# Three small moves of DMA issues in a fused attention-and-MLP kernel: V's parts one per step, w1's quarters on two queues, m0 on a third

## Chip, cores and metric

One Trainium2 chip, one core. The metric is device time in microseconds (us), the median of several executions of the whole program. The span of a profile is shorter than the time of the same execution (before: span 1509.4 us, time 1511.56 us), so spans are compared with spans and times with times.

## The reference, cut to what matters

```python
xn = layernorm(x)                                  # x: 1 x 2048 x 1024, bf16
out = x + A(xn, mem0, Wq, Wk, Wv, Wo, seg_len=32)  # attention by segments of 32 tokens,
                                                   # 32 heads of 128, 8 memory rows handed on
        + B(xn, w1, w2, w3, w4)                    # MLP block
# B begins with  h = gelu(layernorm(xn) @ w1)      # w1: 1024 x 1024
# A, per segment: q, k, v from [mem, xs]; p = softmax(mask(q k^T)); o = p v; o @ Wo
#   mem0: 8 x 1024
```

Everything is on the path somewhere, but TensorE's matrix products are nearly the whole time. The three things that the change touches are loads: `w1` and the first tiles of `x`, `mem0` (called m0 in the kernel), and the tile V, which holds the values of one block of segments for four heads.

## The kernel before

Three places issue the DMAs in question; SyncE (`nc.sync`) issues all of them.

```python
# 1. start: x tiles (128 x 1024) and w1 in quarters, all on SyncE's queue
load_x(0)
for c in range(4):
    nc.sync.dma_start(w1_sb[:, 2 * c:2 * c + 2, :], w1_v[:, 2 * c:2 * c + 2, :])
    if c in (0, 2):
        load_x(1 + c // 2)
# ... statistics, normalisation, transposes of x tile 0 on TensorE, then
def stage1_k(xn2T):              # first product: walks w1's quarters in order
    for k in range(KT):          # KT = 8, two k to a quarter
        if k == KT - 2:
            tr(1, 0); tr(1, 1)   # transposes of x tile 1, ahead of the last quarter
        for co in range(KT):
            nc.tensor.matmul(pss[co // 4][:, co % 4, :], w1_sb[:, k, ...], xn2T[:, 0, k, :], ...)

# 2. between the MLP's stages: 8 rows of memory, ahead of w4
m0 = ring.tile([M, D], BF16, tag="nsq", bufs=1)
nc.sync.dma_start(m0[:], A_mem0[0])

# 3. attention: V's two to four parts in one go
def load_values(B, V, hg):
    for n, i0 in ...:
        nc.sync.dma_start(V[0:w, i0:i0 + k, :], ...)        # token rows, the big part
        if b == 0:
            nc.sync.dma_start(V[96:106, 0, :], Vr_d[0:10, cs_])
        nc.sync.dma_start(V[w:w + n, i0:i0 + k, :], ...)    # memory rows
# ... the attention loop emits one entry of `loads` per step of TensorE work:
loads.append(lambda B=B, V=V, hg=hg: load_values(B, V, hg))
# ... and between the steps each tile's probabilities Pn are transposed by DMA, on SyncE too:
nc.sync.dma_start_transpose(PTr, Pn[:rows]...)              # PT, read by the product with V
```

The last three output stores go to SyncE, SyncE and ScalarE; then a branch follows that is not taken, and the program ends.

```python
for o, q in zip(rest[-3:], (nc.sync, nc.sync, nc.scalar)):
    o.queue = q                  # piece() ends with  queue.dma_start(out_v[...], ot[...])
...
with tc.If(cond > 0):            # line 891 before, 896 after
```

Each DMA that SyncE or ScalarE issues is given one of eight completion counters in turn, in program order, the two engines sharing the eight (read from the semaphores of the DMA instructions in the traces). No line of the source names them.

## Time and profile before

| | before |
|---|---|
| time, 3 runs | 1510.99 us (1510.84 to 1512.13) |
| span of the profile | 1509.4 us |
| PE busy | 1501.7 us |
| waits of PE that the profile lists | 2.9 us |
| of which on DMA: w1 0.8 us, PT 0.4 us | 1.2 us |
| last matmul's end to the end of the span | 4.73 us |

Read it from the top down: PE is busy to within 8 us, and 4.7 of these lie behind its last instruction. The lines for the rows in the middle are in the prediction. For the last row, here is the timeline of all engines at the end of the kernel before (start in us, duration, engine, line, operation; the bracket is the engine's idle time before it). SyncE's last output store at 1501.67 is left out.

```profile
1501.78 2.89 PE L720 MATMUL pso<-wo_sb,oX 128*128 128x256 bf16 x25
...
1504.71 0.42 DVE L726 TENSOR_TENSOR ot<-pso,Rt 128x256 bf16<-128x256 f32 x1 [3.07 <-PE pso L720]
1505.17 0.38 ACTq L727 DMA_DIRECT2D out_dram<-ot  x1
```

The chain at the end is: last matmul, one addition, ScalarE's issue of the last store at 1505.17.

### The profile page before, as it was taken

To read this page: it belongs to the slowest core of one execution; us is meant where nothing else is said; L and a number is where in the kernel's file an instruction comes from. 1 tells how busy PE (TensorE), PEld (TensorE's weight loads), DVE (VectorE), ACT (ScalarE), POOL (GpSimd) and SP (SyncE) were. 2 spreads that over 40 slices of the span, in tenths; PEclk is the share of its full clock that TensorE was granted. 3 is DMA by queue.
4 is the path that set the end of the run, shared out by engine and by line. 5 is a ranking of instruction groups with operands and counts; after the bars stand their busy time and mean duration, and the time that the engine had idled before them with its cause. 6 is when DMAs were issued, how large, how long until landed. Compare 5 with 4: busy or idle time off the path is not lost.

```text
span 1509.4 us, 24313 instructions
## 1 busy us (share of the span) xinstructions
PE 1501.7 (99%) x9834; PEld 803.5 (53%) x9834; DVE 544.8 (36%) x1136; ACT 502.8 (33%) x1140; POOL 175.4 (12%) x245
## 2 busy tenths in 40 slices
PE   9999999999999999999999999999999999999998
PEld 7744444445444444444466645664665455545555
DVE  8382230100020212222146624651664166516641
ACT  6533103013012011111256614650663266416620
POOL 5241020211111221100000010001000100010001
PEclk9999999999999999999999999999999999999999
DMA  9599752353355777522399957992997299918911
GB/s 304 160 252 338 219 177 88 133 203 112 125 165 145 196 252 253 209 98 84 126 229 249 239 129 183 249 240 66 250 244 200 79 223 230 210 60 213 205 46 51
DMA packets 305363, 272.93 MB, mean 181 GB/s; under 512 B 156006, under 2 KB 272264, under 8 KB 305248
## 3 DMA queue, kind: packets, MB, share of 16 engines
q1 hardware_dynamic: 283360, 190.44, 50.7%
q0 software_dynamic: 21744, 80.83, 15.5%
q8 instruction: 79, 1.29, 0.4%
q14 instruction: 36, 0.29, 0.1%
q10 hardware_dynamic: 144, 0.07, 0.0%
HBM read 190.08 MB, written 45.29 MB: 156 GB/s over the span
## 4 chain that ended last, share of the span: by engine, by line
PE 98%; DMA 1%; SPq 0%; issue 0%; DVE 0%
PE ps L662 30%; PE pso L720 15%; PE ps L601 15%; PE ps L542 13%; PE ps L568 13%; PE ps L400 4%; PE ps L318 3%; PE psS L677 2%; PE psO L701 2%; PE ps L860 1%; PE ps L492 1%; DMA PT<-Pn 1%; DMA w_sb<-in_B_w_dram 1%; PE gps L471 0%; PE ps L457 0%; PE ps L295 0%
## 5 line engine op out<-in xcount | busy, mean ns | idle before, releaser
L662 PE MATMUL ps<-hTb,wt 128*128 128x396 bf16 (+2 forms) x2528 | 484.8, 342 | 0.0
L662 PEld LDWEIGHTS <-wt 128*128 128x128 bf16 x2528 | 236.8, 98 | 175.4
L601 PE MATMUL ps<-wt,xT 128*128 128x512 bf16 x1024 | 221.2, 379 | 0.0
L720 PE MATMUL pso<-wo_sb,oX 128*128 128x512 bf16 (+1 forms) x992 | 210.0, 372 | 0.0
L542 PE MATMUL ps<-xn3T,w_sb 128*128 128x512 bf16 x896 | 196.2, 379 | 0.0
L568 PE MATMUL ps<-w_sb,h3T 128*128 128x512 bf16 x896 | 195.5, 379 | 0.0
L601 PEld LDWEIGHTS <-xT 128*128 128x128 bf16 x1024 | 100.2, 98 | 120.8
L543 ACT ACTIVATE h3T<-ps 128x512 bf16<-128x512 f32 x112 | 66.9, 597 | 290.3 <-PE ps L542 289.4
L720 PEld LDWEIGHTS <-oX 128*128 128x128 bf16 x992 | 96.3, 98 | 107.4
L664 ACT CAST KT<-ps 128x462 bf16<-128x462 f32 (+2 forms) x160 | 81.8, 511 | 202.9 <-PE ps L662 198.9
L568 PEld LDWEIGHTS <-h3T 128*128 128x128 bf16 x896 | 87.0, 98 | 103.4
L542 PEld LDWEIGHTS <-w_sb 128*128 128x128 bf16 x896 | 86.6, 98 | 102.1
L683 DVE TENSOR_REDUCE sums<-sm 99x4 f32<-99x396 f32 (+2 forms) x176 | 97.6, 555 | 114.5 <-ACT sm L681 114.5
L666 ACT ACTIVATE QT<-ps 128x462 bf16<-128x462 f32 (+2 forms) x160 | 84.0, 525 | 120.4 <-PE ps L662 106.3
L603 ACT CAST Vs<-ps 128x512 bf16<-128x512 f32 x64 | 37.5, 586 | 233.2 <-PE ps L601 233.2
L679 DVE TENSOR_TENSOR sm<-psS,c_mask_reg_sb 99x396 f32<-99x396 f32 x152 | 86.7, 571 | 72.4 <-PE psS L677 72.2
L607 DVE CAST Vs<-ps 128x512 bf16<-128x512 f32 x64 | 44.3, 692 | 171.6 <-PE ps L601 171.6
L681 ACT ACTIVATE sm<-sm 99x396 f32<-99x396 f32 (+2 forms) x176 | 93.0, 528 | 34.5 <-DVE sm L679 27.6
L689 DVE TENSOR_TENSOR Pn<-sm,rs 99x396 bf16<-99x396 f32 (+2 forms) x176 | 98.9, 562 | 6.9 <-DMA PT<-Pn 1.0
L727 POOL DMA_DIRECT2D out_dram<-ot x30 | 16.4, 547 | 698.6 <-DVE ot L726 692.7
L569 DVE TENSOR_TENSOR R<-ps,R 128x512 f32<-128x512 f32 x32 | 21.9, 689 | 176.0 <-PE ps L568 160.5
L726 DVE TENSOR_TENSOR ot<-pso,Rt 128x512 bf16<-128x512 f32 (+1 forms) x33 | 22.2, 675 | 170.3 <-PE pso L720 166.2
(122 smaller groups left out, 1047.8 us busy)
## 6 DMA issues: line engine op xcount, KB each, us to landing
wt<-in_A_Wq_dram SPq DMA_DIRECT2D x76, 512.0 KB
wt<-in_A_Wk_dram SPq DMA_DIRECT2D x76, 512.0 KB
wt<-in_A_Wv_dram POOLq DMA_DIRECT2D x24, 1024.0 KB, 6.3
V_scratch<-Vs SPq DMA_DIRECT2D x32, 512.0 KB
V<-V_scratch SPq DMA_DIRECT2D x40, 384.0 KB
R_scratch<-x POOLq DMA_DIRECT2D x16, 512.0 KB, 4.1
R<-R_scratch SPq DMA_DIRECT2D x16, 512.0 KB
R_scratch<-R POOLq DMA_DIRECT2D x16, 512.0 KB, 3.6
```

Source lines behind the costliest of these rows:

```text
L542: nc.tensor.matmul(ps[:].rearrange("p (n t) -> p n t", t=P), w3_sb[:, k, f * P:(f + 1) * P], xn3T[tb][:, :, k, :], start=(k == 0), stop=(k ...
L543: nc.scalar.activation(h3T[:, f, :], ps[:], ACTF.Gelu_apprx_tanh)
L568: nc.tensor.matmul(ps[:], h3T[:, f, j * P:(j + 1) * P], w4_sb[:, f, ch * 512:(ch + 1) * 512], start=(f == 0), stop=(f == FT - 1))
L601: nc.tensor.matmul(ps[:], xT[:, m4 * 4 + j, k, :], wv[:, k, :], start=(k == 0), stop=(k == KT - 1))
L662: nc.tensor.matmul(ps[:, :nb], w[:, k, hh * P:(hh + 1) * P], B["hT"][:, k, :nb], start=(k == 0), stop=(k == KT - 1))
L664: nc.scalar.copy(dst[:, hh, :], ps[:, :nb])
L666: nc.scalar.mul(dst[:, hh, :], ps[:, :nb], scale)
L679: nc.vector.tensor_tensor(sm[:T, :, :T], S3, t["mask"][:].unsqueeze(1).to_broadcast((T, 4, T)), op=ALU.add)
L681: nc.scalar.activation(e[:T, :, :T], sm[:T, :, :T], ACTF.Exp, scale=LN2)
L683: nc.vector.tensor_reduce(ss, e[:T, :, :T], axis=AX.X, op=ALU.add)
L689: nc.vector.tensor_tensor(Pn[:T, :, :T], e[:T, :, :T], rs[:T, :].unsqueeze(2).to_broadcast((T, 4, T)), op=ALU.mult)
L720: nc.tensor.matmul(self.ps[:, :self.w], self.oX[0][:, h, self.oX[1] + self.gl * P:self.oX[1] + (self.gl + 1) * P], wo_sb[:, h, self.cc], s ...
```

## The change

Its intent: let two queues bring w1 in, so that fewer loads stand one behind the other at the start; take a small load off SyncE ahead of w4; and put V's parts at separate steps, so that a transpose of probabilities that TensorE will wait for does not queue behind all of them.

```diff
-for c in range(4):
-    nc.sync.dma_start(w1_sb[:, 2 * c:2 * c + 2, :], w1_v[:, 2 * c:2 * c + 2, :])
-    if c in (0, 2):
+for c, q in ((0, nc.scalar), (2, nc.scalar), (1, nc.sync), (3, nc.sync)):
+    if q is nc.sync:
         load_x(1 + c // 2)
+    q.dma_start(w1_sb[:, 2 * c:2 * c + 2, :], w1_v[:, 2 * c:2 * c + 2, :])
@@
-nc.sync.dma_start(m0[:], A_mem0[0])
+nc.gpsimd.dma_start(m0[:], A_mem0[0])
@@
-def load_values(B, V, hg):          # issues V's parts itself
+def value_loads(B, V, hg):          # returns one function for each part
+    def add(dst, src):
+        out_.append(lambda: nc.sync.dma_start(dst, src))
     ...                             # the same parts, nc.sync.dma_start(...) -> add(...)
+    return out_
@@
-    loads.append(lambda B=B, V=V, hg=hg: load_values(B, V, hg))
+    loads += value_loads(B, V, hg)
```

TensorE's instruction order is the same in both programs, and no arithmetic is added or removed.

More of the change, by code (lines that the diff above doesn't have):

```diff
@@ L645, in block_setup @@
             return dict(b=b, tiles=tl, nb=nb, ntok=ntok, hT=hTb)
-        def load_values(B, V, hg):
-            b, cs_ = B["b"], slice(hg * 512, (hg + 1) * 512)
+        def value_loads(B, V, hg):
+            b, cs_, out_ = B["b"], slice(hg * 512, (hg + 1) * 512), []
+            def add(dst, src):
+                out_.append(lambda: nc.sync.dma_start(dst, src))
             for n, i0 in ((3, int(b == 4)),) + (((2, 4 if b == 3 else 0),) if b > 2 else ()):
@@ L651, in load_values @@
                 r, w = SEG * t["seg"], SEG * n
-                nc.sync.dma_start(V[0:w, i0:i0 + k, :], V_d[r:r + w * k, cs_].rearrange("(t p) c -> p t c", p=w))
+                add(V[0:w, i0:i0 + k, :], V_d[r:r + w * k, cs_].rearrange("(t p) c -> p t c", p=w))
                 if b == 0:
-                    nc.sync.dma_start(V[96:106, 0, :], Vr_d[0:10, cs_])
+                    add(V[96:106, 0, :], Vr_d[0:10, cs_])
                     i0, k, t = 1, 3, B["tiles"][1]
-                nc.sync.dma_start(V[w:w + n, i0:i0 + k, :], Vr_d[t["r0"]:t["r0"] + n * k, cs_].rearrange("(t j) c -> j t c", j=n))
+                add(V[w:w + n, i0:i0 + k, :], Vr_d[t["r0"]:t["r0"] + n * k, cs_].rearrange("(t j) c -> j t c", j=n))
+            return out_
         def proj(B, w, hh, dst, scale):
```

## The prediction

> **What bounds the kernel now.** I read the head of the page first, with its busy row, clock row and DMA queues.
>
> ```profile
> span 1509.4 us, 24313 instructions
> ...
> PE 1501.7 (99%) x9834; PEld 803.5 (53%) x9834; DVE 544.8 (36%) x1136; ACT 502.8 (33%) x1140; POOL 175.4 (12%) x245
> ...
> PEclk9999999999999999999999999999999999999999
> ...
> q1 hardware_dynamic: 283360, 190.44, 50.7%
> ...
> q10 hardware_dynamic: 144, 0.07, 0.0%
> ```
>
> TensorE (PE) is busy 1501.7 of 1509.4 us, at full granted clock in every slice. The DMA queue of ScalarE (q10) carries almost nothing, 0.07 MB; nearly all of SyncE's and hence of the kernel's loads go through q1. Busy is not the same as fast, so the second view is PE's timeline in the middle of the MLP, where each row is a run of matmuls that nothing interrupts.
>
> ```profile
> 122.30 48.51 PE L542 MATMUL ps<-xn3T,w_sb 128*128 128x512 bf16 x224
> 170.65 48.51 PE L568 MATMUL ps<-w_sb,h3T 128*128 128x512 bf16 x224
> ```
>
> From the start of the first run to the start of the second are 48.35 us for 224 matmuls of 512 columns: 215.8 ns each. There is no slack inside a busy stretch. The page's mean of 379 ns for the same matmuls counts the overlap of neighbours twice and must not be multiplied by their count. So only PE's idle time can be won, and the third view, who PE waited for, holds all of it (total us, times, longest).
>
> ```profile
> PE warm L335 <- DVE wz L329: 1.4, 1, 1.4
> PE ps L308 <- DMA w_sb<-in_B_w_dram: 0.8, 2, 0.5
> PE psO L701 <- DMA PT<-Pn: 0.4, 1, 0.4
> PE ps L295 <- DVE xn L274: 0.3, 1, 0.3
> ```
>
> The listed waits sum to 2.9 us. Of these the first, 1.4 us, is program start, and the last, 0.3 us, is the normalisation of the first x tile. What DMA can be blamed for is 0.8 us on w1 (named w_sb here; line L308 is the first stage-1 product, which walks w1's quarters in order) and 0.4 us on one transposed probability tile PT. The rest of the 7.7 us between busy and span is the end: PE's last matmul ends at 1504.7 us, and output store and final semaphores follow until 1509.4. The change touches none of that. The fourth view is PE's timeline at the start (start, duration; the bracket is the idle time before).
>
> ```profile
> 6.57 0.72 PE L295 MATMUL ps<-c_ident_sb,xn 128*128 128x128 bf16 x8 [0.29 <-DVE xn L274]
> 7.43 1.96 PE L308 MATMUL ps<-xn2T,w_sb 128*128 128x128 bf16 x32
> 9.69 1.07 PE L308 MATMUL ps<-xn2T,w_sb 128*128 128x128 bf16 x16 [0.30 <-DMA w_sb<-in_B_w_dram]
> 10.59 0.61 PE L295 MATMUL ps<-c_ident_sb,xn 128*128 128x128 bf16 x8
> 11.72 1.07 PE L308 MATMUL ps<-xn2T,w_sb 128*128 128x128 bf16 x16 [0.52 <-DMA w_sb<-in_B_w_dram]
> ```
>
> Sixteen matmuls belong to one quarter of w1, so quarters 1 and 2 run at 7.43 without a wait, the third waits 0.30 us and the fourth 0.52 us (before it PE does the second tile's transposes, 10.59). The fifth view asks whether those two quarters are late because they were issued late or because the DMA engines were full (last two columns: mean share of the 16 engines busy, GB/s).
>
> ```profile
> 2.00:4.00 2.00, 2.00 (x6) 0.67 (x5) 0.53 (x1) 0.24 (x2) 0.61 (x1) 1.00 0.98 226
> 4.00:6.00 2.00, 2.00 (x7) 0.65 (x5) 1.19 (x4) 0.00 (x0) 0.66 (x1) 1.00 0.91 349
> 6.00:8.00 2.00, 1.57 (x21) 1.08 (x20) 1.74 (x4) 0.99 (x4) 0.07 (x1) 1.00 1.01 340
> 8.00:10.00 2.00, 1.70 (x31) 1.52 (x29) 1.11 (x4) 0.21 (x1) 1.14 (x4) 1.00 1.06 409
> ```
>
> The engines are 91 to 106% busy from 2 us on, but deliver only 226 GB/s in the first window and about 345 in the next two, against 409 later. SyncE had issued the fourth quarter by 4.7 us (issue at 4.01, 0.68 us long), seven microseconds before PE got it. Late data, then, not late issue. The last view is SyncE's own timeline ahead of the single PT wait (PE at 797.12).
>
> ```profile
> 786.97 1.15 SPq L652 DMA_DIRECT2D V<-V_scratch  x1
> 788.16 0.70 SPq L654 DMA_DIRECT2D V<-Vmem_scratch  x1
> 788.92 0.26 SPq L656 DMA_DIRECT2D V<-Vmem_scratch  x1
> 789.28 2.61 SPq L692 DMA_TRANSPOSE PT<-Pn  x1
> ```
>
> The transpose at 789.28 is the one that PE waits for; its tile Pn was finished at 787.2 (VectorE started it at 786.64 for 0.57 us), and SyncE was then busy with the three parts of V.
>
> **What the Trainium skill says.** "DMA: Bandwidth & Descriptors", section "Issuing engines are not separate DMA queues": DMAs started from different engines run on the same 16 DMA engines and interleave, and a second issuer saves only the issue time. The windows above agree as far as they can: full engines while one queue issues. The same page, "Queues, rings and completion order": each DMA engine takes turns between the queue rows that have work, packet by packet. No trace of the kernel before shows two loaded hardware queues, so the sharing below is an estimate resting on that sentence. "TensorE: Matmul & The Clock Gate", section "Wait — 56ns, not 53.3ns?", gives 215.7 ns between warm 512-column matmuls; the trace has 215.8, so PE's stretches are at their floor.
>
> **The change part by part.** Comparing the two programs with line numbers aligned, PE's instruction order is identical and so are ScalarE's except for two DMA issues at its head; no arithmetic is added or removed. The base of the sum is therefore the old time, 1510.99 us.
>
> (1) w1 on two queues. On one queue the order is x0, q0, x1, q1, q2, x2, q3 (x tile 256 KB, quarter 512 KB), so these are complete after 256, 768, 1024, 1536, 2048, 2304 and 2816 KB. Adding up the trace's packet records on q1 gives when each amount was across: 2.96, 4.90, 5.71, 7.29, 8.68, 9.33, 10.62 us; PE sees a quarter about 1.0 us later (q2: 8.68 to 9.69; q3: 10.62 to 11.72). After the change ScalarE issues q0, q2 and SyncE x0, x1, q1, x2, q3. With equal turns x0 is complete at 512 KB, q0 and x1 at 1024, q1 and q2 together at 2048, x2 at 2304, q3 at 2816. Thus q2, x2 and q3 gain nothing, while x0 and q1 lose.
> - Same delivery as before: x0 lands at about 3.9 us (between 2.96 at 256 KB and 4.90 at 768) instead of 2.96. The chain that it feeds (statistics from 3.47, transposes at 6.57, first product at 7.43) moves to about 8.4. q1, at 2048 KB, is visible at 9.7. Then q1 and q2 run 9.7 to 11.7, the transposes to 12.2, and q3, there since 11.7, starts at 12.2 instead of 11.72: plus 0.5 us.
> - Two queues fill the start: if from 1.8 us (first packet 1.77) the engines deliver 400 GB/s, 2048 KB are across at 7.0 and 2816 KB at 9.0 us. Both w1 waits, 0.82 us, vanish; x0 costs some 0.15 us. Minus 0.7 us.
> The slow start consists of packets that took 400 to 1000 ns instead of the usual 84, at the first touch of x0 and w1, and these may partly overlap on two queues. I put the mean at minus 0.1 us. ScalarE's two issues cost about 0.9 us at its head (SyncE's took 0.42 and 0.47 each), before its 1.28 us table load; it is first needed at 7.01, so this is beside the path.
>
> (2) m0 moved to GpSimd's queue: 0.62 us of issue leave SyncE at 130.5 us. The w4 loads behind it feed products from 170.65 us, and PE does not wait there. VectorE swaps one xr sum (2.35 us for two) with the first R addition (180.49 us); the PSUM buffer that this addition frees is wanted again at 194.8 us (176.7 plus three groups of 6.05), so zero.
>
> (3) V's parts one per step. Same bytes, same number of DMAs; only which of them stands between two PT transposes changes. Of the row of three, the two small ones (0.70 + 0.26 us) go behind the next transpose, so a transpose leaves up to 1.0 us earlier. The one wait is 0.36 us, so the gain is at most that; but the 384 KB part stays ahead of it on the same queue, and the issue-to-use time was 7.7 us, most of it moving data. I count minus 0.15. V itself comes a few steps later, some 1.5 us each; the products that read it are scheduled 10 to 12 us after their scores, so no new wait is expected.
>
> Sum: 1510.99 - 0.1 + 0 - 0.15 = 1510.7 us.
>
> **The rivals.** (a) The x0 chain and q1 become the first wait: for it speaks the byte count, against it only the slow first packets. It makes 1511.3 to 1511.5. If PE's idle stretch before the first product also brought the clock down (the warm-up matmuls, 4.91 us for 12, ran at about half speed), another 1 to 2 us: 1513. (b) Everything is won: w1 waits and PT wait gone, 1510.99 - 0.82 - 0.36 = 1509.8. For it speaks that 226 GB/s leaves room; against it that the engines were already marked busy. (c) The shifted transposes make new waits of a few tenths in the first block, where loads and transposes share a queue at over 100% busy share: 1511 to 1512. No rival reaches 2%, which is 30 us; all PE idle time of the old trace together is a tenth of that.
>
> **Range and chances.** The effects span -1.2 to +1 us, and the three old runs alone spread from 1510.84 to 1512.13. I say 1510.7 us, range 1509.3 to 1512.3. Faster by over 2%: 0.01; within 2%: 0.98; slower by over 2%: 0.01.
>
> **What would show it.** In the new profile PE stays at about 1501 us busy. Step 1: q10 carries about 1.1 MB; PE's waits on w_sb either shrink below 0.8 us in total (fill) or a wait appears at the second quarter and the first product moves from 7.43 past 8 us (sharing). If the time between first packet and 2816 KB is unchanged at about 8.8 us, queues do not add delivery. Step 3: the PT wait of 0.4 us goes or stays below 0.4, and no psO wait over 0.5 us is new. I would be wrong if PE's total idle grew by more than 2 us, or if matmul cadence changed anywhere.

## The result, and the profile after

| | before | after |
|---|---|---|
| time, 6 runs each | 1511.05 us (1510.12 to 1512.14) | 1510.68 us (1510.15 to 1511.5) |
| ratio, 95% interval | | 0.9997 (0.9984 to 1.001): same |
| span of the profile | 1509.41 us | 1508.11 us |

Here and below a ratio is the mean time of one kernel's fast runs over that of the other's in the same rounds, so not quite the ratio of the medians that are quoted.

The time is where the prediction put it. The traces say whether for its reasons. First the head of the page of the changed kernel.

```profile
span 1508.1 us, 24241 instructions
...
PE 1498.3 (99%) x9762; PEld 803.5 (53%) x9834; DVE 544.6 (36%) x1136; ACT 501.9 (33%) x1140; POOL 175.6 (12%) x246
...
q10 hardware_dynamic: 688, 1.11, 0.2%
```

ScalarE's queue q10 now carries 1.11 MB, as intended. PE's busy time is 3.4 us lower, but this is no gain: 72 matmul records are missing (9762 against 9834, while the weight loads are 9834 in both). PE's totals can't be compared here, only times at which a given weight load starts. Done so, by the number of the weight load, the 1.30 us between the spans divide up as follows.

| stretch | before, us | after, us | difference |
|---|---|---|---|
| start to the first product's first weight load | 7.07 | 7.69 | +0.62 |
| from there to the first weight load after the first product | 5.50 | 4.32 | -1.18 |
| near 31.6 us (x tile 7's transposed tile lands later) | | | +0.16 |
| attention, the stretch of the PT wait (787.6 to 798.3) | 10.68 | 10.72 | +0.04 |
| last matmul's end to the end of the span | 4.73 | 3.80 | -0.94 |

The first two rows are step 1 of the prediction. PE's timeline at the start of the changed kernel:

```profile
7.19 0.72 PE L295 MATMUL ps<-c_ident_sb,xn 128*128 128x128 bf16 x8 [0.51 <-DVE xn L274]
8.04 2.84 PE L308 MATMUL ps<-xn2T,w_sb 128*128 128x128 bf16 x48
10.72 0.61 PE L295 MATMUL ps<-c_ident_sb,xn 128*128 128x128 bf16 x8
11.17 1.06 PE L308 MATMUL ps<-xn2T,w_sb 128*128 128x128 bf16 x16
```

The first product starts at 8.04 instead of 7.43 us, and then runs three quarters (x48) and the fourth (x16) without a wait on w1. VectorE's first use of x tile 0 tells why it starts later. Here is that row, of before and then of after:

```profile
3.47 0.69 DVE L259 BATCH_NORM_STATS2 st<-xt 128x6 f32<-128x512 bf16 x1 [2.15 <-DMA xt<-in_A_x_dram]
```

```profile
4.08 0.69 DVE L259 BATCH_NORM_STATS2 st<-xt 128x6 f32<-128x512 bf16 x1 [2.76 <-DMA xt<-in_A_x_dram]
```

x tile 0 arrives 0.61 us later, because it now shares the DMA engines with the first quarter of w1: by 4.0 us the packet records have 256 KB, all of x tile 0, across on SyncE's queue and 296 KB on ScalarE's. And the windows of the changed kernel (the last two columns are DMA share and GB/s):

```profile
2.00:4.00 2.00, 2.00 (x6) 0.69 (x5) 0.00 (x0) 1.25 (x2) 0.60 (x1) 1.00 0.93 275
4.00:6.00 2.00, 2.00 (x6) 0.68 (x5) 1.72 (x4) 0.00 (x0) 0.04 (x1) 1.00 1.06 404
6.00:8.00 2.00, 1.40 (x10) 0.51 (x9) 1.28 (x4) 0.38 (x2) 0.68 (x1) 1.00 1.03 383
```

275, 404 and 383 GB/s stand against 226, 349 and 340 before. On these two traces alone one would say: two queues fill the engines better, and this pays for the later x tile. The experiments test that.

Step 3, SyncE's timeline ahead of the PT transpose:

```profile
786.84 1.24 SPq L651 DMA_DIRECT2D V<-V_scratch  x1
788.19 2.10 SPq L697 DMA_TRANSPOSE PT<-Pn  x1
790.33 0.83 SPq L651 DMA_DIRECT2D V<-Vmem_scratch  x2
```

The transpose leaves at 788.19 instead of 789.28, right behind the big part of V, and the two small parts come after it. This is what the change meant to do. PE's wait there shrinks from 0.36 to 0.13 us, but a wait of 0.10 us on a Wq tile appears at 789.6 us.

The last row was not in the prediction. The end of the changed kernel:

```profile
1501.74 2.57 PE L725 MATMUL pso<-wo_sb,oX 128*128 128x256 bf16 x22
...
1504.35 0.42 DVE L731 TENSOR_TENSOR ot<-pso,Rt 128x256 bf16<-128x256 f32 x1 [3.07 <-PE pso L725]
1504.80 0.37 ACTq L732 DMA_DIRECT2D out_dram<-ot  x1
```

The same chain, with the same durations, 0.36 us earlier. But the span ends 1.30 us earlier: from the issue of the last store to the end it takes 3.30 us instead of 4.24. The records of SyncE's sequencer, which the timeline does not print, show how. SyncE checks the eight completion counters one after the other before the program may end (start of each check in us, one of SyncE's waits on a semaphore, counted here from 0 in the order of the checks; the last line is the end of the span):

```
before              after
1506.77 counter 0   1501.92 counter 0
1506.87 counter 1   1502.02 counter 1
1506.96 counter 2   1502.11 counter 2
1507.37 counter 3   1502.19 counter 3
1507.46 counter 4   1502.26 counter 4
1507.54 counter 5   1502.34 counter 5
1507.62 counter 6   1502.88 counter 6
1507.69 counter 7   1506.39 counter 7
1509.41 end         1508.11 end
```

Before, the last store is counted on counter 0. SyncE waits at its first check until that store has landed, 1.60 us after its issue (1505.17 to 1506.77; the counter's last update is recorded at 1506.75), and has the other seven checks still ahead of it. After, the last store is on counter 7: seven checks are done while TensorE is still at work, the eighth waits for the store (1504.80 to 1506.39, 1.59 us), and what follows is the same as before, 1.72 us. The seven checks are 0.92 us. The reason is the giving out in turn: m0 on GpSimd's queue means one DMA fewer among those of SyncE and ScalarE, so every later one gets the counter before its own, and the last store moves from 0 to 7.

That the store is felt only 1.6 us after its issue fits the Trainium skill, "Perfetto Trace Analysis", section "DMA Instruction — HWDGE (DVE, Sync)": the counter is written after the data write is confirmed, which can take surprisingly long when the target is HBM.

### The profile page after: what moved, and what is told of

It reads as the page before. It is cut to its first block, busy times and chain, and to the rows that moved or that the text cites. A ratio compares the mean times of both kernels' runs of the same rounds, so it can differ in the third digit from the quotient of the medians.

```text
span 1508.1 us, 24241 instructions
## 1 busy us (share of the span) xinstructions
PE 1498.3 (99%) x9762; PEld 803.5 (53%) x9834; DVE 544.6 (36%) x1136; ACT 501.9 (33%) x1140; POOL 175.6 (12%) x246
## 3 DMA queue, kind: packets, MB, share of 16 engines
q10 hardware_dynamic: 688, 1.11, 0.2%
## 4 chain that ended last, share of the span: by engine, by line
PE 97%; DVE 1%; DMA 1%; issue 0%; POOL 0%; ACT 0%; SPq 0%; POOLq 0%
PE ps L667 30%; PE pso L725 15%; PE ps L601 15%; PE ps L542 13%; PE ps L568 13%; PE ps L400 4%; PE ps L318 2%; PE psS L682 2%; PE psO L706 2%; PE ps L865 1%; PE ps L492 1%; PE gps L471 0%; PE ps L457 0%; DMA wt<-in_A_Wq_dram 0%; DVE st L262 0%
```

## The experiments

The theory after this reading: (T1) the end is the only lasting effect, 0.93 us, and follows from the last store's counter; (T2) two queues deliver w1 faster, net minus 0.5 us at the start; (T3) V's parts save a few tenths. The rival to all three: differences of half a microsecond between two traces are chance, since a trace is one execution. Eleven runs were made, two of them of the unaltered kernels; all were correct, and all were timed in rounds beside the kernel before. "End" is always from the last matmul's end to the end of the span; "x0" is when VectorE first reads x tile 0; "first product" is the time of the first weight load after it, 12.57 us before and 12.01 us after.

### One part at a time

**w1_only.** The kernel before with the first hunk alone.

```diff
+for c, q in ((0, nc.scalar), (2, nc.scalar), (1, nc.sync), (3, nc.sync)):
```

> The kernel before with only w1 on two queues; m0 stays with SyncE, V in one step. The program gives the last store DMA completion counter 0 of the 8 that SyncE and ScalarE share, as in the kernel before (counter 7 in the changed kernel). Three-causes theory (head, V, end are separate): first stage-1 product at 8.0 us, no w1 wait on PE, PE 0.56 us ahead at the first single-matmul product and 0.40 us ahead after tile 7; the PT wait near 797 stays at 0.2 to 0.5 us; the end from PE's last matmul to the last instruction stays at 4.7 us; span about 1509.0. Rival (w1's queues did it all): span 1508.1, end 3.8 us. Rival (end is chance): end anywhere between 3.8 and 4.7.

Measured: 1511.5 us (1510.57 to 1512.45) against 1511.18 for the kernel before, ratio 1.0001 (0.9987 to 1.0014). End 4.725, as before. x0 at 3.86, first product done at 11.78, PE's lead over the first trace 0.79 us there and 0.63 us at the last matmul: more than the changed kernel's 0.56 and 0.36. In time there is no gain at all, so PE's lead over that one trace is not yet a lead over the kernel before.

**m0_only.** The second hunk alone.

```diff
-nc.sync.dma_start(m0[:], A_mem0[0])
+nc.gpsimd.dma_start(m0[:], A_mem0[0])
```

> The kernel before with only m0 moved to GpSimd's queue. It has one hardware-queue DMA less, so the last store takes completion counter 7, which SyncE checks last. Three-causes theory: PE's timeline as before to within 0.05 us (w1 waits 0.30 and 0.52, PT wait 0.36, last matmul ends at 1504.7), but the end shrinks from 4.73 to about 3.8 us, span 1508.5, time 0.9 us below before. Rival (moving m0 is worth nothing, as the prediction counted): end 4.7 us, span 1509.4.

Measured: 1510.02 us (1509.6 to 1511.52), ratio 0.9992 (0.9979 to 1.0006). End 3.791, as T1 says. The expectation for PE missed: w1 is still on one queue here, and yet PE has no wait on w1, and the first product is done at 11.69, earlier than with two queues. So the 0.82 us of w1 waits belonged to the first trace, not to the kernel.

**v_only.** The third hunk alone.

```diff
-    loads.append(lambda B=B, V=V, hg=hg: load_values(B, V, hg))
+    loads += value_loads(B, V, hg)
```

> The kernel before with only V's parts at separate steps. Three-causes theory: head as before, end 4.7 us; near 797 the 0.36 us PT wait shrinks to about 0.1 but a wait on Wq or on the next PT near 790 of 0.1 to 0.3 us takes its place, so PE's last matmul ends within 0.1 us of 1504.67. Prediction's step 3: the wait only shrinks, last matmul 0.15 us earlier (up to 0.36). Span 1509.2 to 1509.5 in either.

Measured: 1510.56 us (1510.03 to 1512.11), ratio 0.9993 (0.9979 to 1.0006). End 4.730. Two rows of PE's timeline show what V's parts did in this run:

```profile
790.32 0.86 PE L667 MATMUL ps<-hTb,wt 128*128 128x403 bf16 x4 [0.60 <-DMA wt<-in_A_Wq_dram]
...
797.63 0.34 PE L706 MATMUL psO<-PT,V 99*128 99x99 bf16 x4 [0.25 <-DMA PT<-Pn]
```

The PT wait is 0.25 instead of 0.36, and a wait of 0.60 on a Wq tile is new. PE also waited 0.36 us at 39 us and 0.20 us at 1291 us, places that do not stand in the first trace. Both expectations for PE missed: its last matmul ends at 1505.53, 0.86 us later than in the first trace and not 0 to 0.36 us earlier, and the span is 1510.26.

**again.** The changed kernel, unaltered.

> The changed kernel unaltered, to see what repeats. If the differences of the two traces are the program's and not the run's: first product at 8.0, PE 0.56 ahead then 0.40, last matmul at 1504.3, end 3.8 us, all within 0.1 us of the first trace. If they are chance, they differ by as much as 0.5 us. Time against before, 5 rounds: minus 0.9 to minus 1.3 us if the trace's span gain (1.30 us) is what the clock measures, minus 0.4 or less if not.

Measured: 1509.56 us (1509.34 to 1510.54), ratio 0.9988 (0.9974 to 1.0001). End 3.794, x0 at 4.01, first product done at 11.94: these repeat to 0.07 us. But the last matmul ends at 1504.81, 0.50 us later than in the first trace of the same kernel, because PE waited 0.56 us at 39 us. The expectation of 0.1 us was missed by that: one trace does not tell half a microsecond in PE's total. The time lies 1.6 us below the kernel before in the same rounds, more than the 0.9 to 1.3 us expected.

### The same kernel twice, and the counter by itself

**before_again.** The kernel before, unaltered, timed against itself.

> The kernel before unaltered, timed against itself: what chance alone does. If the w1 waits (0.30 and 0.52 us) of its first trace belong to the program, they are here again within 0.1 us. If they belong to that run (the two kernels with w1 on one queue that ran since, m0 alone and V alone, showed none), they are absent, the 2 to 8 us windows deliver over 340 GB/s and PE is 0.7 to 0.9 us ahead of the first trace at the end of the first product. The end stays at 4.73 us in both. Ratio of times 1.000, and its interval shows what three rounds can tell.

Measured: 1511.36 us (1511.02 to 1511.87) against 1510.93, ratio 1.0001 (0.9985 to 1.0016). End 4.730. PE's timeline and the windows of this second trace of the kernel before:

```profile
7.50 2.84 PE L308 MATMUL ps<-xn2T,w_sb 128*128 128x128 bf16 x48
10.18 0.61 PE L295 MATMUL ps<-c_ident_sb,xn 128*128 128x128 bf16 x8
10.88 1.07 PE L308 MATMUL ps<-xn2T,w_sb 128*128 128x128 bf16 x16
```

```profile
2.00:4.00 2.00, 2.00 (x6) 0.67 (x5) 0.45 (x1) 0.24 (x2) 0.61 (x1) 1.00 0.99 245
4.00:6.00 2.00, 2.00 (x7) 0.64 (x5) 1.26 (x4) 0.00 (x0) 0.58 (x1) 1.00 1.05 400
6.00:8.00 2.00, 1.47 (x19) 1.00 (x18) 1.82 (x4) 0.92 (x4) 0.14 (x1) 1.00 1.04 386
```

With one queue, three quarters run without a break (x48), and the engines deliver 245, 400 and 386 GB/s where the first trace of the very same program had 226, 349 and 340. Nearly all of the delivery that looked like the work of the second queue is there without it, so the first pair of traces does not show T2. How much of it is left is counted over all traces below.

**m0_rows.** The kernel before with m0 left on SyncE, but in eight DMAs of a row. That is seven DMAs more, so the last store goes from counter 0 to 7 while m0's queue stays.

```diff
-nc.sync.dma_start(m0[:], A_mem0[0])
+for r in range(M):
+    nc.sync.dma_start(m0[r:r + 1, :], A_mem0[0][r:r + 1, :])
```

> The kernel before with m0 loaded on SyncE's queue as before, but in eight DMAs of one row: seven more hardware-queue DMAs, so the last store takes completion counter 7 though nothing left SyncE's queue. Counter theory: end of 3.8 us, time 0.9 us below before, as with m0 on GpSimd. Rival (the gain comes from taking m0 off SyncE): end of 4.7 us, time as before or above.

Measured: 1510.57 us (1509.14 to 1511.01), ratio 0.9993 (0.9979 to 1.0006). The end of its timeline, with a span of 1508.79:

```profile
1501.76 3.22 PE L721 MATMUL pso<-wo_sb,oX 128*128 128x256 bf16 x28
...
1505.47 0.38 ACTq L728 DMA_DIRECT2D out_dram<-ot  x1
```

From the issue to the end of the span are 3.31 us, against 4.24 in the kernel before and 3.30 in the changed one; the end is 3.807. More DMAs, on the same queue, with the same gain: it is the counter, not m0's queue.

**m0_pairs.** Four DMAs of two rows: three more, so the last store gets counter 3.

```diff
+for r in range(0, M, 2):
+    nc.sync.dma_start(m0[r:r + 2, :], A_mem0[0][r:r + 2, :])
```

> The same with four DMAs of two rows: three more hardware-queue DMAs, the last store on counter 3 of 0 to 7. Counter theory: SyncE has four counters left to check after the one that it waits for, 0.08 us each: an end of 4.1 us, up to 4.5 if the 0.4 us step between its third and fourth check comes after it. Rival (chance or m0's queue): 4.7 or 3.8 us.

Measured: 1510.43 us (1510.18 to 1510.66), ratio 0.9993 (0.9978 to 1.0009). End 4.114: between the two others. The sequencer's records show the checks 0 to 2 done by 1503.13, the fourth waiting until 1506.63, and the other four at 0.07 to 0.09 us each. So four checks behind the landing take 0.30 us, where seven took 0.92 in the kernel before. That is less than four sevenths because the kernel before has one slow step of 0.40 us among its seven (counter 2 to 3); what makes it slow is not shown. Here a step of 0.40 us (counter 0 to 1) falls ahead of the wait, where it costs nothing. The step of 0.59 us after it is itself a wait: for the last store but one, which is on counter 2, was issued at 1501.52 and landed 1.6 us later.

**act_late.** The changed kernel with ScalarE's two w1 DMAs behind its table load instead of ahead of it, to give x tile 0 a start.

```diff
 nc.scalar.activation(gtab[:], ones_f[:], ACTF.Gelu_apprx_tanh)
+for c in (0, 2):
+    nc.scalar.dma_start(w1_sb[:, 2 * c:2 * c + 2, :], w1_v[:, 2 * c:2 * c + 2, :])
```

> The changed kernel with ScalarE's two w1 DMAs issued after its table load and first activation (about 2.3 us) instead of before. Sharing theory (x0 is late because it takes turns with q0): x0 is seen at 3.5 us as on one queue, not 3.9 to 4.1, the first product is at 7.4 to 7.7 instead of 7.8 to 8.0, no w1 wait. Whether PE keeps the gain depends on the transposes near 31 and 39 us: 0 to 0.5 us. Rival (x0's delay is chance): x0 at 3.9 us or later. End 3.8 us.

Measured: 1509.9 us (1509.51 to 1511.27), ratio 0.9993 (0.9979 to 1.0006). End 3.794.

```profile
7.68 1.05 PE L307 MATMUL ps<-xn2T,w_sb 128*128 128x128 bf16 x16
8.89 1.96 PE L307 MATMUL ps<-xn2T,w_sb 128*128 128x128 bf16 x32 [0.15 <-DMA w_sb<-in_B_w_dram]
```

x0 comes at 3.72 instead of 4.0, between the two expectations, but now the second quarter is waited for, 0.15 us, against the expectation, and the first product is done at 11.97, no earlier. The second quarter came no later than it had: its counter is full at 8.84 us here and at 8.78 in the changed kernel. The product starts earlier and so meets it.

### Two parts at a time

**m0_v** is the changed kernel with w1 back on one queue, **m0_w1** with V in one step, **w1_v** with m0 back on SyncE.

```diff
 m0_v:   -for c, q in ((0, nc.scalar), ...      +for c in range(4):   (the loop of before)
 m0_w1:  -    loads += value_loads(B, V, hg)    +    loads.append(lambda ...: load_values(...))
 w1_v:   -nc.gpsimd.dma_start(m0[:], ...)       +nc.sync.dma_start(m0[:], ...)
```

> The changed kernel with w1 back on SyncE's queue alone. Counter theory: end 3.8 us, time 0.9 us below before. x0 seen at 3.4 to 3.75 us as in the six traces with w1 on one queue. V theory (separate parts shorten the PT wait near 797): that wait is below 0.33 us, where the six traces with V in one step had 0.33 to 0.80 and the four with separate parts 0.29 or less; a Wq wait of up to 0.6 us near 790 may come beside it. Rival (the PT wait is chance): 0.33 us or more. If w1 on two queues helps, this kernel is slower than the changed one's minus 0.4 to minus 1.6; I expect no difference.

> The changed kernel with V's parts in one step again. V theory: the PT wait near 797 is 0.33 us or more. Rival: below that. x0 seen at 3.8 to 4.1 us, end 3.8 us, time 0.5 to 1.3 us below before.

> The changed kernel with m0 back on SyncE's queue, so the last store is on counter 0 again. Counter theory: end 4.73 us and a time within 0.5 us of before, although w1 and V are changed. Rival (w1 and V carry the gain): end 3.8 us or time 0.9 us below before. PT wait below 0.33 us, x0 at 3.8 to 4.1 us.

| | time, us | before, same rounds | ratio (95%) | end | x0 | first product |
|---|---|---|---|---|---|---|
| m0_v | 1510.53 (1509.73 to 1511.51) | 1511.16 | 0.9996 (0.9983 to 1.001) | 3.782 | 3.62 | 12.09 |
| m0_w1 | 1510.37 (1509.8 to 1510.8) | 1511.16 | 0.9994 (0.9979 to 1.0009) | 3.793 | 3.99 | 11.91 |
| w1_v | 1510.94 (1510.09 to 1516.23) | 1511.16 | 1.0007 (0.9989 to 1.0024) | 4.724 | 3.98 | 11.90 |

The end goes with m0 alone, a third time. The PT waits are 0.20, 0.56 and 0.25 us, on the sides of 0.33 us that were expected of separate parts, of one step and of separate parts again. The 1516.23 of w1_v is one outlier of four runs and is explained by nothing here. In m0_w1 there is a trap in reading waits:

```profile
796.80 0.34 PE L701 MATMUL psO<-PT,V 99*128 99x99 bf16 x4 [0.56 <-ACT KT L664]
```

The profile puts this wait, at the place of the PT wait, down to a cast of KT on ScalarE that ended at 796.78. But this matmul reads PT and V, not KT; and in the kernel before PE went on at 797.12 while the same cast ran from 796.80 to 797.30. The cast ended just then by accident. The records of PE's sequencer settle it: ahead of this matmul it waits for the counter of the transpose that SyncE issued at 788.89, whose last update came at 796.66, and it goes on at 796.69. PT was awaited here as elsewhere.

### All thirteen traces together

| | traces | values, us | mean |
|---|---|---|---|
| end, last store on counter 0 | 5 | 4.72 to 4.73 | 4.73 |
| end, counter 3 | 1 | 4.11 | |
| end, counter 7 | 7 | 3.78 to 3.81 | 3.79 |
| x0, w1 on one queue | 7 | 3.47 to 3.73 | 3.57 |
| x0, w1 on two queues from the start | 5 | 3.86 to 4.08 | 3.98 |
| first product done, one queue | 7 | 11.68 to 12.57 | 11.98 |
| first product done, two queues from the start | 5 | 11.78 to 12.01 | 11.91 |
| first packet until 2816 KB are across, one queue | 7 | 8.27 to 8.85 | 8.46 |
| the same, two queues from the start | 5 | 8.13 to 8.20 | 8.17 |
| wait at the PT place, V in one step | 7 | 0.33 to 0.80 | 0.53 |
| the same, V's parts separate | 6 | 0 to 0.29 | 0.19 |
| the whole stretch 787.6 to 798.3, V in one step | 7 | 10.65 to 11.38 | 10.94 |
| the same, V's parts separate | 6 | 10.16 to 11.35 | 10.72 |
| last matmul's end, all | 13 | 1503.85 to 1505.53 | |

- T1 stands. The groups of the end do not touch, and in time the seven kernels with counter 7 have a mean of 1510.34 us over 35 runs, those with counter 0 of 1511.21 us over 50 (without the outlier): 0.87 us. The standard errors are 0.11 and 0.10; kernels and chips are mixed in both groups, so this supports the 0.93 us of the traces rather than measuring it.
- T2 holds for the delivery, and smaller than thought, but not for TensorE. The DMA packets of both hardware queues, added up, bring the first 2816 KB in 0.29 us less on average with two queues, and the groups do not touch, if barely (8.20 and 8.27 us). By the counters w1's last quarter lands at 10.71 us on average instead of 11.07, but the second at 8.68 instead of 7.68. TensorE has little of it: the later x tile is certain, 0.4 us, and the means for the first product differ by 0.08 us in a spread of 0.9. What two queues may also do is make the start more even: 0.23 us of spread against 0.89.
- T3 is half shown. The PT wait is shorter by 0.34 us and the groups do not overlap. Waits on a Wq tile in the same stretch come with both forms (0.10 and 0.60 us in two of the six with separate parts, 0.09 us in `m0_rows` and `m0_pairs`), so only the 0.60 of `v_only` might be the change's. Over the whole stretch the gain is 0.2 us with a spread larger than that.
- The rival is right for PE's total: with the same order of instructions on PE, its last matmul ends anywhere within 1.7 us.

One thing stays open. Four of the six traces with V's parts separate have a wait of 0.36 to 0.59 us at 39 us, and none of the seven others has one. 39 us is far ahead of any of V's loads, and two other traces with separate parts lack it. Nothing in the runs connects the two.

No version is clearly better than the changed kernel. `m0_only`, with one line of the change, has its whole measured gain.

## Why the prediction was right or wrong, point by point

**The total was right:** 1510.7 us predicted, 1510.68 measured, within the range of 1509.3 to 1512.3, and "same" at 0.98. Its reasons were right only in part, and the median falls on the sum partly by luck: the later rounds of the changed kernel gave 1509.56, and those of its variants with the same end 1509.9 to 1510.53.

**The step that failed: "output store and final semaphores follow until 1509.4. The change touches none of that."** It does. The end went from 4.73 to 3.80 us, the largest lasting effect of the change, because of the step (2) that was counted as zero: m0 leaves the queues that share the eight counters. The prediction looked at what m0's move does to SyncE's time and VectorE's order, where it is indeed worth nothing, and not at the end, which had 4.7 us in it, more than all of PE's listed waits together.

**Step 1, w1 on two queues, minus 0.1 us:** nothing contradicts the value (0.08 us at the first product, in a spread of 0.9), but the ground under it does not hold. The sharing was seen as predicted: x tile 0 is later by 0.4 us on average, between the 0.15 of the fill case and the 0.94 of equal turns at the old delivery, and the second quarter is later too, by 1.0 us. That the third and fourth quarters gain nothing was wrong: they land 0.74 and 0.36 us earlier on average. The prediction's own test, the time from the first packet to 2816 KB, gave 8.20 us instead of 8.85; the second trace of the kernel before has 8.38, so most of this was chance and some of it the second queue. The prediction took the w1 waits of 0.30 and 0.52 us as the kernel's own. They were one execution's: six other traces with one queue have 0 to 0.42 us. The delivery of 226 to 349 GB/s was this execution's too. Rival (b), which wins all 0.82 us, had 0.24 us to win on average over the seven traces, against an x tile that comes 0.4 us later. The forecast sign of "two queues fill the start", shrinking waits, did appear in the changed kernel's trace and would have confirmed a gain that the runs do not show.

**Step 2:** zero for the path between is right: no trace has a wait of TensorE over 0.15 us between m0's load and the attention. Minus 0.93 us at the end was missed.

**Step 3, V's parts, minus 0.15 us:** the mechanism held, the transpose left earlier (788.19 instead of 789.28, of which 0.40 is PE's own lead at that point), and the PT wait fell by 0.34 us on average. The size was capped by one trace's wait of 0.36 us; the average of seven is 0.53. V itself was waited for in no trace, as expected; whether the one large Wq wait (0.60 us) comes of the change is not settled. Net, the predicted 0.15 us lies within what the stretch shows, 0.2 us with a spread larger than that.

**Rivals:** of (a), the later x0 chain occurred (0.4 us), but the wait on the second quarter did not, except in `act_late`, and the clock did not drop as its worse form feared: the weight loads of the first product stay 0.056 us apart (the median) in all thirteen traces, also behind an idle stretch of 1.15 us (`w1_v`). (c), new waits of tenths: the traces with separate parts do have some, at 39 us and once on Wq, but they come and go between executions of one kernel. Neither is visible in the time.

## What to carry to other kernels

When a kernel is within a few us of its bound, look at the whole stretch behind the last instruction too: the rows end with the last store, but the program ends only when the completion counters have been checked one by one, and here a DMA added to or taken from SyncE and ScalarE anywhere earlier shifted which of them the last store used. Take a second trace of the unchanged kernel before explaining a difference of half a microsecond; here it removed the very waits that the change was meant to cure. A second queue shifts who gets the data first: here the first 2816 KB came some 0.3 us sooner, x tile 0 came 0.4 us later, and the time did not change measurably.

## What the Trainium skill lacked or had wrong

- "Runtime: NRT & Kernel Launch", section "The ~15µs preamble/postamble breakdown", lists barrier and semaphore resets after the kernel, but no page has the checks of the DMA completion counters ahead of them, nor that their order against the last store matters: with seven checks behind the landing the end is 0.93 us longer than with none (4.73 against 3.79 us in 5 and 7 traces).
- "DMA: Bandwidth & Descriptors", section "Issuing engines are not separate DMA queues", is borne out in the time (no gain from the second issuer), though the first 2816 KB were across 0.29 us sooner on average; the section leaves out the price: the first tile on the other queue came 0.4 us later.
- No page says how much the delivery of a program's first loads varies: the same kernel was given 340 and 386 GB/s in the same window (6 to 8 us) of two executions, and had 0.82 and 0.08 us of waits on w1.
